# Amplitude copies moved behind their transposes, and the side jobs of a convolution and FFN kernel put in another order

## The chip, the cores and the metric

The kernel runs on one core of a Trainium2 chip. The metric is the device time of one execution in microseconds (us): 1000.81 us before, the median of three runs (998.63 to 1002.74). A core has five engines that run their own instruction streams and wait for one another by semaphores: PE (TensorE, matmuls), DVE (VectorE), ACT (ScalarE, with function tables that must be loaded), POOL (GpSimd) and SP (SyncE, which here issues DMAs).

## What is computed

A block of a sequence model with 2048 rows of 640 columns: a layer norm with a modulation from a condition vector, a convolution with a state-space kernel K (640 channels, 192 modes each), a residual, a second layer norm, and a gated FFN without a nonlinearity (640 to 1536 to 640).

```python
mod = (_silu(c) @ w_mod).reshape(c.shape[0], 6, 1, -1)
sa, ca, ga, sb, cb, gb = (mod[:, i] for i in range(6))
h = _layernorm(x) * (1 + ca) + sa
# _A_ref: dt = exp(log_dt); P = exp(dt * (A_re + 1j*A_im) * l), l = 0..2047
K = jnp.einsum("dn,dnl,dn->dl", Cc, P, dB).real
y = irfft2(rfft2(pad(h)) * rfft2(pad(K)))[:L] + h * Dskip
x = x + ga * y
h = _layernorm(x) * (1 + cb) + sb
x = x + gb * (((h @ w_gate) * (h @ w_up)) @ w_down)
```

## The kernel before

**Generating K.** The 640 channels go in five blocks of 128, db 0 to 4. Each block has two halves, hf 0 to 9, and each half four steps, so that n runs from 0 to 39 (NK = 40). For each n, a value exp(a·l)·sin or cos(b·l) is put together from small tables. `u_seeds(db)` makes the seeds of a block from the inputs A, B and C in steps named by letters: s_d (bit fields of the phase, L689 to L696), s_r (multiples of the decay rate, L702 and L704), s_x, s_e (the exponentials, on ACT), s_f (amplitude `amp` and the input `y` of an arctan, L729 to L734), s_g (transposes of `amp` on PE, then the arctan on ACT), s_h (transposes of the arctan) and s_v (copies of the transposed amplitude into the fourth row of the tile RL, L759, and the phase offset `psi`, L760). The transposes are L639 to L641. The strings SEG0 (block 0) and SEG (the others) group the letters into pieces that are placed one by one.

From the seeds, POOL makes tables: `tab_ph(hf)` the phase table LH (L808 to L814, L789), `tab_eq(hf)` the narrow amplitude table LQ (L823, L824, L789) and, for every n, three outer products on one line, L829: the phases Pha or Phb, EQ (from LQ) and EP (from LP). There are two buffers of each.

**The loop.** `for t in range(3*NK+24)` has three phases per n. ACT takes sines of the phases into the tiles tra and trb (`kg_aq`, `kg_ap`, `kg_b`). DVE multiplies them with EQ and EP to QtA (L884), PtA (L890), PtB (L910) and QtB (L884). PE multiplies these into kg (L925 for the A tiles, L940 for the B tiles), and POOL makes the phases, EQ and EP of n + 1.

**Side jobs.** Everything else is put into this loop as side jobs: seeds of the next block, layer-norm statistics, the modulation, and the convolution itself. Its jobs are `u_pre` (first stage of the input's transform, L986, loads hf), `u_k` (first stage for K, L962), `u_g` and `u_c` (second stages, L1007; `u_c` multiplies the two spectra on DVE, L1048 to L1054, and goes back with L1067) and `u_d` (last stage, L1117 and L1122). Where each piece stands is a number in the table SCHED: 1000 times the half phase of the loop (`due(2t)` stands in front of DVE's multiplies, `due(2t+1)` behind them), plus its place among the jobs there; negative numbers lie in the prologue. The buffers are picked by letters in the table SLOT: `psf` names the PSUM banks a, b and c, `tr` ACT's result tiles, and so on. `mark` and `need` are assertions on the order of the program text; they make no wait. The streams are issued in program order, and semaphores follow from the buffers.

After n = 39 the FFN follows: products of the gate and up weights' halves (L1208) and the down projection (L1624) on PE, with products on DVE and POOL.

Of the kernel before, what the change touches and what calls it, by code (L numbers as in the profile page):

```python
# [14 lines left out]
OP = mybir.AluOpType  # L15
# [17 lines left out]
    ml=(8000, 2001, -93999),  # L33
    mr=(((8004, 13001), (8002, 12000)), ((2002, 8001), (7000, 8003)), ((1, 2000), (-87000, 11004))),
    st=(
        (-96000, -86994),
        (-98000, -86996),
        (2, 12001),
        (2003, 5000),
        (-94999, 4000),  # L40
        (-94000, -86999),
        (14002, 17001),
        (-99999, 0),
        (8005, 8007),
        (-88000, -86995),
        (14003, 18000),
        (8006, 11005),
        (-100000, -86997),
        (-95000, -91000),
        (11000, 11003),  # L50
        (11002, 13002),
    ),
    hm=(
        (29000, 29000),
        (26001, 26001),
        (17000, 17000),
        (32000, 32000),
        (15000, 15000),
        (23000, 23000),
        (22003, 25000),  # L60
        (22001, 27000),
        (35009, 46000),
        (11006, 24002),
        (34000, 36000),
        (32001, 35006),
        (29001, 33000),
        (16001, 20000),
        (43003, 54001),
        (37000, 51002),
    ),  # L70
    rstd=(12002, 18001),
    tab=(52005, 68003),
    fo=(14000, 14001, 14004, 20001),
    e0=(-86998,),
    mc=((11001, 26000, 31002, 34003, 34004), (13000, 35001, 45000, 50000, 51001), (35002, 59000, 63001)),
    q=(
# [4 lines left out]
    ),  # L81
    pre=(
# [8 lines left out]
            (105002, 105004, 108001, 109000),  # L91
            (79000, 81002, 96000, 99000),
            (93001, 93003, 110001, 110002),
            (80001, 82001, 93000, 93002),
        ),
        (
            (139001, 139004, 143000, 144000),
            (132000, 133001, 134010, 139002),
            (119001, 119002, 131000, 132001),
            (111000, 111001, 121000, 123001),  # L100
        ),
        (
            (190003, 192002, 202001, 204000),
            (157000, 157001, 164000, 166002),
            (165000, 167001, 178006, 182004),
            (187003, 187004, 199002, 200000),
        ),
        (
            (207000, 209001, 212001, 215000),
            (220000, 222000, 226000, 229002),  # L110
            (229000, 229001, 232002, 233003),
            (233000, 233004, 236000, 239000),
# [21 lines left out]
        (24001, 26002),  # L134
        (34001, 34002),
        (67001, 69002),
        (51003, 52001),
        (43000, 43004),
        (43002, 46002),
        (52000, 52003),  # L140
        (52002, 52004),
        (66003, 68007),
        (81003, 83000),
        (86002, 92000),
        (108000, 108002),
        (94000, 94001),
        (95000, 95001),
        (105000, 105001),
        (105005, 107000),
        (127000, 127001),  # L150
        (123000, 125006),
        (140000, 144002),
        (134009, 139000),
        (150002, 150004),
        (139003, 140001),
        (150003, 152002),
        (150000, 152001),
        (160001, 162002),
        (166003, 166004),
        (190000, 190002),  # L160
        (192000, 193000),
        (194002, 196000),
        (199001, 199003),
        (196002, 196003),
        (196001, 196004),
# [149 lines left out]
def tile_kernel(ctx: ExitStack, tc: tile.TileContext, I, out):  # L315
# [293 lines left out]
    def u_seeds(db):  # L609
# [22 lines left out]
        T = {}  # L632
# [1158 lines left out]
```

## Time and profile before

| | |
|---|---|
| median of three runs | 1000.81 us (998.63 to 1002.74) |
| the profiled execution | 1001.23 us, of which the span is 999.4 us |
| busy share of the span | PE 90%, DVE 76%, ACT 58%, POOL 58% |
| mean granted TensorE clock | 0.96 of full speed |
| generating K and the convolution | 0 to about 521 us; PE busy 426 us of it |
| FFN | about 521 us to the end; PE busy 468 of 478 us |

Rows of a timeline read: start in us, duration in us (of the whole group, if a count follows as x2), engine, line, operation, the tile written and the tiles read, shapes; in brackets at the end, how long the engine had been idle before it and what ended the idle time. Rows of windows read: start and end, length, then for PE, PEld (weight loads), DVE, ACT and POOL the busy time and the number of instructions, then the granted clock of TensorE, the DMA share and GB/s. A wait's row reads: engine, tile and line that waited, what it waited for, then the total in us, the count and the longest.

### The profile page before, as it was taken

How to read it: one execution, taken by the hardware profiler on the slowest of the kernel's cores; microseconds unless marked ns; L12 is line 12 of the kernel's file. 1: busy time of each engine (PE TensorE's matmuls, PEld its weight loads, DVE VectorE, ACT ScalarE, POOL GpSimd, SP SyncE). 2: the span in 40 equal slices, each digit the busy share in tenths (PEclk: the TensorE clock that was granted, in tenths of full speed). 3: DMA queues.
4: the chain of work that ended last, by engine and by line, in shares of the span. 5: the costliest groups of instructions: out<-in, count | busy, mean ns of one | idle time of the engine just before them, and what ended most of it. 6: DMA issues, size and time to landing. Idle time of an engine off the chain costs nothing.

```text
span 999.4 us, 26670 instructions
## 1 busy us (share of the span) xinstructions
PE 894.6 (90%) x11190; PEld 728.3 (73%) x11190; DVE 760.6 (76%) x1319; ACT 581.7 (58%) x1020; POOL 577.5 (58%) x424
## 2 busy tenths in 40 slices
PE   3966786998798789999878999999999999999998
PEld 2654555775475476677656888889998888889998
DVE  8996678886978977897889877687576877768352
ACT  7789888886978887974564222234463422224331
POOL 5997998799679969970046667650112354442000
PEclk9969999999989979999989999999999999999999
DMA  8756554534365634649741542534645232212341
GB/s 282 280 192 206 167 178 169 159 99 139 108 193 147 178 101 122 183 135 307 223 113 54 192 150 88 185 131 136 224 142 192 101 102 79 80 53 63 95 160 53
DMA packets 141177, 148.96 MB, mean 149 GB/s; under 512 B 8192, under 2 KB 119296, under 8 KB 139648
## 3 DMA queue, kind: packets, MB, share of 16 engines
q1 hardware_dynamic: 139904, 146.32, 46.6%
q8 instruction: 88, 1.44, 0.6%
q10 hardware_dynamic: 1152, 0.92, 0.3%
q14 instruction: 33, 0.27, 0.1%
HBM read 108.36 MB, written 38.86 MB: 147 GB/s over the span
## 4 chain that ended last, share of the span: by engine, by line
PE 64%; ACT 10%; DVE 9%; POOL 7%; issue 5%; DMA 3%; SPq 0%; DVEq 0%; ACTq 0%; POOLq 0%
PE pa L1208 26%; PE pa L1624 16%; PE psfc L1007 2%; PE kg L925 2%; PE kg L940 2%; PE psfa L1007 2%; PE psfb L1007 2%; POOL EQ L829 2%; PE psfa L986 1%; PE psfa L1067 1%; DVE QtA L884 1%; ACT trb L320 1%; ACT tra L320 1%; POOL Phb L829 1%; POOL LH L789 1%
## 5 line engine op out<-in xcount | busy, mean ns | idle before, releaser
L829 POOL TENSOR_TENSOR EQ<-LQ,RH 128x1536 f32<-128x1536 f32 x40 | 124.1, 3102 | 8.5 <-DVE QtB L884 8.3
L320 ACT ACTIVATE z<-pa 128x512 f32<-128x512 f32 x24 | 14.4, 599 | 165.8 <-PE pa L1208 120.1
L1172 DVE TENSOR_TENSOR wsgl<-wga,wsgh 128x640 fp32r<-128x640 f32 x72 | 68.3, 950 | 46.6 <-ACT wsgh L320 46.3
L320 ACT ACTIVATE wsgh<-wga 128x640 fp32r<-128x640 f32 x72 | 52.5, 731 | 72.9 <-PE pa L1624 41.8
L1573 POOL TENSOR_TENSOR z<-z,s 128x512 f32<-128x512 f32 x24 | 33.4, 1391 | 98.8 <-DVE s L1572 98.8
L1624 PE MATMUL pa<-wsgh,sh 128*128 128x384 f32 (+1 forms) x304 | 69.6, 310 | 0.0
L829 POOL TENSOR_TENSOR Pha<-LH,DH 128x1536 int32<-128x1536 int32 x20 | 62.2, 3112 | 12.1 <-ACT tra L320 12.1
L1624 PE MATMUL pa<-wsgl,sh 128*128 128x384 f32 (+1 forms) x304 | 69.2, 309 | 0.0
L1624 PE MATMUL pa<-wsgh,sl 128*128 128x384 f32 (+1 forms) x304 | 69.2, 309 | 0.0
L1184 POOL TENSOR_TENSOR tf<-wur,wgb 128x256 f32<-128x256 f32 x24 | 19.3, 802 | 81.0 <-DVE wtl L1172 54.4
L829 POOL TENSOR_TENSOR EP<-LP,RH 128x768 f32<-128x768 f32 x40 | 66.0, 1649 | 0.0
L829 POOL TENSOR_TENSOR Phb<-LH,DH 128x1536 int32<-128x1536 int32 (+1 forms) x21 | 62.4, 2972 | 3.5 <-ACT trb L320 3.0
L884 DVE TENSOR_TENSOR QtA<-trb,EQ 128x1024 f32<-128x1024 f32 x40 | 47.0, 1215 | 18.9 <-PE kg L925 15.8
L1172 DVE TENSOR_TENSOR wtl<-tf,wth 128x256 fp32r<-128x256 f32 (+1 forms) x72 | 59.9, 859 | 0.0
L884 DVE TENSOR_TENSOR QtA<-tra,EQ 128x1024 f32<-128x1024 f32 x40 | 47.0, 1215 | 13.6 <-ACT tra L320 4.8
L1571 DVE TENSOR_TENSOR s<-pa,s 128x512 f32<-128x512 f32 x24 | 16.6, 691 | 45.1 <-PE pa L1208 40.0
L940 PE MATMUL kg<-QtB,PtB 64*32 64x64 f32 x2560 | 46.5, 224 | 1.4 <-issue 1.0
L1208 PE MATMUL pa<-sl,wth 128*128 128x512 f32 x144 | 45.1, 395 | 2.1 <-DVE sl L1172 2.1
L940 PEld LDWEIGHTS kg<-QtB,PtB 64*32 64x32 f32 x2560 | 39.6, 111 | 9.3 <-issue 6.0
L1624 PEld LDWEIGHTS pa<-wsgh,sh 128*128 128x128 f32 x304 | 46.4, 188 | 0.0
L1624 PEld LDWEIGHTS pa<-wsgh,sl 128*128 128x128 f32 x304 | 46.4, 188 | 0.0
L1624 PEld LDWEIGHTS pa<-wsgl,sh 128*128 128x128 f32 x304 | 46.4, 188 | 0.0
(610 smaller groups left out, 2941.8 us busy)
## 6 DMA issues: line engine op xcount, KB each, us to landing
wga<-wdg SPq DMA_DIRECT2D x24, 640.0 KB, 4.4
wga<-B_w_gate SPq DMA_DIRECT2D x12, 640.0 KB, 5.8
wgb<-B_w_gate SPq DMA_DIRECT2D x24, 320.0 KB, 3.4
wur<-B_w_up SPq DMA_DIRECT2D x24, 320.0 KB, 4.0
xb<-x2d SPq DMA_DIRECT2D x6, 1280.0 KB, 7.2
TVb<-WD SPq DMA_DIRECT2D x20, 256.0 KB, 3.5
t_tw<-w_mod SPq DMA_DIRECT2D x3, 1600.0 KB, 9.2
t_ti<-w_mod SPq DMA_DIRECT2D x3, 1600.0 KB, 8.9
```

Source lines behind the costliest of these rows:

```text
L320: return S.activation(o, i, f, **kw)
L829: G.tensor_tensor(o.rearrange("p x (h l) -> p x h l", l=8), lo.unsqueeze(2).to_broadcast([P, rows, nh, 8]), hi.rearrange("p h x -> p x h") ...
L884: return [lambda h=h: V.tensor_tensor(Qt[:, :, :, 32 * h : 32 * h + 32], tr[:, ::-1] if h else tr[:, :, :, ::-1], e[:, :, 32 * h : 32 * h ...
L925: PE.matmul(kg[j * 32 : j * 32 + 32, dd, :], PtA[:, c, dl * 4 + j, :], QtA[:, c, dl * 4 + j, :], start=dd == 0 and c == 0, stop=False, til ...
L940: PE.matmul(kg[j * 32 : j * 32 + 32, dd, :], PtB[lo : lo + 64, c, r, :], QtB[lo : lo + 64, c, r, :], start=False, stop=dd == 7 and c == 1, ...
L1007: PE.matmul(r[c][par * 64 : par * 64 + 64, i, :], t_tw[:, k0 + k, c, :], src[:, k, :], start=True, stop=True, tile_position=(0, par * 64))
L1172: V.tensor_tensor(lo, v, hi, op=OP.subtract)
L1184: G.tensor_tensor(t[:, 0:2], u[:, 0:2], g[:, 0:2], op=OP.subtract)
L1208: PE.matmul(ps, w[a][:, k], x[b][:, l], start=n == 0 and m == 0, stop=n == 2 and m == len(ks) - 1)
L1571: V.tensor_tensor(S67[i], ps, S6[i], op=OP.add)
L1573: G.tensor_tensor(ZT[i], ZT[i], S67[i], op=OP.add)
L1624: PE.matmul(ACC[tb][t][c], x[:, ts], w[:, cs], start=st, stop=f == NF - 1 and n == 2 and (c == 0 or t % 2 == 1))
```

## The change

Four things change. In `s_f` the amplitude moves from the first to the last place of its six operations. The copies of the transposed amplitude move from `s_v` to `s_g`, directly behind the amplitude's transposes and ahead of the arctan (for block 0 they stood there already, on ACT). `tab_eq` asks for these copies alone (the new mark "amps") and no longer for the whole of the seeds. And nearly all numbers of SCHED and letters of SLOT are others; among them e0, the exponentials of half 1, move from the prologue to the first phase of the loop. Lines from L747 on have a number one higher after the change, so that L884 becomes L885; the five operations behind `amp` become L729 to L733, `amp` L734 and the copies L752.

```diff
-    e0=(-86998,),
+    e0=(2,),
...
-            V.scalar_tensor_tensor(amp, u, dt2[:, db : db + 1], pe[:, 1], op0=OP.mult, op1=OP.mult)
             V.scalar_tensor_tensor(pe[:, 0], pe[:, 0], 1e-37, u, op0=OP.max, op1=OP.add)
             V.reciprocal(pe[:, 0], pe[:, 0])
             V.scalar_tensor_tensor(y, y, 2.0, pe[:, 1], op0=OP.mult, op1=OP.mult)
             V.tensor_tensor(pe[:, 0], y, pe[:, 0], op=OP.mult)
             V.tensor_scalar(y, pe[:, 0], 1.0, -1.0, op0=OP.min, op1=OP.max)
+            V.scalar_tensor_tensor(amp, u, dt2[:, db : db + 1], pe[:, 1], op0=OP.mult, op1=OP.mult)
...
                 for h in range(2):
                     act(g4(Rl[h])[:, 3], T["ps2"][:, 0, hs[h]])
+                mark("amps", db)
...
             if db:
                 s_G()
+                for h in range(2):
+                    V.tensor_copy(g4(Rl[h])[:, 3], T["ps2"][:, 0, hs[h]])
+                mark("amps", db)
             act(y, y, AF.Arctan)
...
             ps = T["ps2"]
-            if db:
-                for h in range(2):
-                    V.tensor_copy(g4(Rl[h])[:, 3], ps[:, 0, hs[h]])
             V.tensor_scalar(psi, ps[:, 1], 4294967296.0 / math.pi, 536870912.0, op0=OP.mult, op1=OP.add)
...
-        need(1, "seeds", hf // 2)
+        need(1, "amps", hf // 2)
```

What the new numbers do is shown at three places.

The first is ACT at n = 13, where the seeds of block 2 are made. `ab`, `tra` and `trb` are the sines' tiles, `ptb` and `psfa` the square root and absolute value of the seeds, LP, RH and RL the exponentials. Before:

```order
L320 ACTIVATE gha<-psfb 128x512
L320 ACT_TABLE_LOAD
L320 ACTIVATE ptb<-ptb 128x192
L320 ACTIVATE psfa<-ptb 128x192
L320 ACT_TABLE_LOAD
L320 ACTIVATE LP<-RL 128x192 x7
L320 ACTIVATE RH<-RH 128x2112
L320 ACTIVATE RL<-RL 128x2x288
L320 ACTIVATE ab<-Pha 128x512
L320 ACT_TABLE_LOAD
L320 ACTIVATE tra<-Pha 128x512
L320 ACTIVATE tra<-ab,halfpi 128x512
```

And now:

```order
L320 ACTIVATE ab<-Phb 128x512
L320 ACTIVATE trb<-Phb 128x512
L320 ACTIVATE trb<-ab,halfpi 128x512
L320 ACT_TABLE_LOAD
L320 ACTIVATE ptb<-ptb 128x192
L320 ACTIVATE psfc<-ptb 128x192
L320 ACT_TABLE_LOAD
L320 ACTIVATE LP<-RL 128x192 x7
L320 ACTIVATE RH<-RH 128x2112
L320 ACTIVATE RL<-RL 128x2x288
```

The third set of sines of n = 13 has moved from behind the exponentials to a place ahead of them and of the square root. On DVE, at the same n, the first of the two product groups (six operations each) has moved ahead of L714, and `amp` stands last of its group; both product groups still stand ahead of PtB and QtB.

The second place is DVE at n = 22, where the seeds of block 3 are finished (`psfa` and `psfc` are PSUM banks, `prm` holds `amp`, `pta` the arctan's input and TVb the spectra's product). Before, from L714 to the copies:

```order
L714 TENSOR_SCALAR psfa<-ptb 128x192
L884 TENSOR_TENSOR QtA<-trb,EQ_144 128x32x32 x2
L1048 TENSOR_TENSOR TVb<-psfb,gha 128x512
...
L1054 TENSOR_TENSOR TVb<-TVb,psfc 128x512
L729 SCALAR_TENSOR_TENSOR prm<-ptb,dt_100,psfa 128x192
L730 SCALAR_TENSOR_TENSOR psfa<-psfa,ptb 128x192
L731 RECIPROCAL psfa<-psfa 128x192
L732 SCALAR_TENSOR_TENSOR pta<-pta,psfa 128x192
L733 TENSOR_TENSOR psfa<-pta,psfa 128x192
L734 TENSOR_SCALAR pta<-psfa 128x192
L759 COPY RL<-psfa 128x96 x2
L760 TENSOR_SCALAR ptb<-psfa 128x192
```

And now, from QtA on:

```order
L885 TENSOR_TENSOR QtA<-tra,EQ_144 128x32x32 x2
L1049 TENSOR_TENSOR TVb<-psfb,ghc 128x512
...
L1055 TENSOR_TENSOR TVb<-TVb,psfa 128x512
L714 TENSOR_SCALAR psfc<-ptb 128x192
L729 SCALAR_TENSOR_TENSOR psfc<-psfc,ptb 128x192
L730 RECIPROCAL psfc<-psfc 128x192
...
L733 TENSOR_SCALAR pta<-psfc 128x192
L734 SCALAR_TENSOR_TENSOR prm<-ptb,dt_100,psfc 128x192
L752 COPY RL<-psfc 128x96 x2
L891 TENSOR_TENSOR PtAb<-trb,EP_146 128x1024
L761 TENSOR_SCALAR ptb<-psfc 128x192
```

L714 has moved behind QtA and the product group, `amp` to the end of its group, and PtA stands between the copies and psi.

The third place is n = 29, where the seeds of block 4 are finished, on DVE and on PE. On DVE, before:

```order
L890 TENSOR_TENSOR PtAa<-trb,EP_147 128x1024
L714 TENSOR_SCALAR psfa<-ptb 128x192
L729 SCALAR_TENSOR_TENSOR prm<-ptb,dt_100,psfa 128x192
...
L734 TENSOR_SCALAR pta<-psfa 128x192
L910 TENSOR_TENSOR PtB<-tra,EP_147 128x512
L884 TENSOR_TENSOR QtB<-tra,EQ_145 128x16x32 x2
L884 TENSOR_TENSOR QtA<-trb,EQ_144 128x32x32 x2
L759 COPY RL<-psfa 128x96 x2
```

And now:

```order
L891 TENSOR_TENSOR PtAa<-tra,EP_147 128x1024
L911 TENSOR_TENSOR PtB<-trb,EP_147 128x512
L885 TENSOR_TENSOR QtB<-trb,EQ_145 128x16x32 x2
L714 TENSOR_SCALAR psfc<-ptb 128x192
L1123 TENSOR_TENSOR xsa<-psfa,xsa 128x512
...
L734 SCALAR_TENSOR_TENSOR prm<-ptb,dt_100,psfc 128x192
L885 TENSOR_TENSOR QtA<-tra,EQ_144 128x32x32 x2
L752 COPY RL<-psfa 128x96 x2
```

PtB and QtB of n = 29 have moved ahead of L714 and the six operations. On PE, behind the L1117 group of n = 28, before:

```order
L940 MATMUL kg<-QtB,PtB 32x64 x32
L1117 MATMUL psfa<-TVb,ct 32x512 x4
L1007 MATMUL psfc<-ghc,t_tw 64x128 x2
...
L1067 MATMUL psfb<-TVa,t_ti 128x128
L925 MATMUL kg<-QtA,PtAa 32x64 x32
L929 MATMUL kg<-dsel,jsel 128x8
```

And now:

```order
L1118 MATMUL psfa<-TVb,ct 32x512 x4
L926 MATMUL kg<-QtA,PtAa 32x64 x32
L930 MATMUL kg<-dsel,jsel 128x8
L1008 MATMUL psfb<-ghb,t_tw 64x128 x2
...
L941 MATMUL kg<-QtB,PtB 32x64 x32
L1068 MATMUL psfc<-TVa,t_ti 128x128
```

The L925 block of n = 29 has moved ahead of the L1007 block, and the L1067 block to a place behind L940; the amplitude's transposes (L639) come behind these as before.

More of the change, by code (lines that the diff above doesn't have):

```diff
@@ L133 @@
     k=(
[L134 to L146, printed above, removed]
-        (95000, 95001),
[L148 to L165, printed above, removed]
-        (208001, 211001),
-        (233001, 237000),
-        (220001, 224005),
-        (229003, 229004),
+        (20000, 25000),
+        (35010, 36002),
+        (67008, 68000),
+        (53000, 57000),
+        (40001, 42002),
+        (40000, 43001),
+        (56001, 59000),
+        (52000, 53001),
+        (67004, 67005),
+        (82002, 82003),
+        (90001, 93000),
+        (104000, 107000),
+        (95000, 95001),
+        (96000, 96001),
+        (103003, 105000),
+        (103006, 106000),
+        (128002, 128003),
+        (128000, 128001),
+        (143000, 143001),
+        (136000, 140000),
+        (156000, 156002),
+        (140002, 140004),
+        (148000, 150000),
+        (159000, 159003),
+        (160000, 162002),
+        (169000, 169001),
+        (187004, 190000),
+        (189001, 193000),
+        (203000, 203001),
+        (200000, 200001),
+        (198000, 198001),
+        (196000, 197000),
+        (210002, 210004),
+        (233004, 233005),
+        (220000, 224000),
+        (231000, 231001),
         (287007, 287017),
@@ L175 @@
     low=(
-        (15001, 43005, 64000, 90003, 110000, 139005, 160000, 187005, 211002),
-        (16000, 43001, 68000, 90005, 116000, 136000, 162000, 187002, 211000),
+        (14000, 43000, 66000, 88005, 115001, 136003, 162001, 187005, 206000),
+        (16000, 42000, 67007, 88003, 112000, 136001, 164001, 187003, 209001),
     ),
```

130 lines of the change are left out of this document (65 added, 65 removed), and 34 rows, old and new, of tables (d, g, pre, q).

## The prediction

> **What bounds the kernel now.** I read the chain of waits first, then the windows, then the list of POOL's waits, then the timeline at the five places where seeds are made. The chain ends on PE:
>
> ```profile
> PE 64%; ACT 10%; DVE 9%; POOL 7%; issue 5%; DMA 3%; SPq 0%; DVEq 0%; ACTq 0%; POOLq 0%
> ```
>
> The windows (start, length, then busy time and count of PE, PEld, DVE, ACT, POOL) show where that holds:
>
> ```profile
> 25.00:75.00 50.00, 39.88 (x641) 30.91 (x640) 46.58 (x108) 42.10 (x70) 49.13 (x28) 0.80 0.69 236
> 75.00:120.00 45.00, 31.32 (x618) 21.87 (x620) 27.84 (x43) 42.14 (x67) 38.87 (x26) 0.93 0.56 181
> 375.00:521.00 146.00, 131.02 (x2620) 99.26 (x2620) 117.72 (x229) 97.84 (x166) 77.24 (x48) 0.96 0.59 177
> 521.00:999.00 478.00, 468.35 (x2464) 411.92 (x2462) 338.29 (x532) 170.81 (x330) 179.95 (x162) 0.99 0.38 122
> ```
>
> From 521 us on PE is busy 468.35 of 478, and the diff leaves that part's order alone: it can only move as a block. Before it, POOL (49.13 of 50) and then ACT (42.14 of 45) are fuller than PE, and each n must pass POOL's EQ and EP. So what the change is worth is the sum of POOL's waits that go or come before its last EP, unless PE cannot follow. POOL's largest waits in the table stage are (total, times, longest):
>
> ```profile
> POOL LQ L823 <- DVE RL L759: 14.2, 3, 9.6
> POOL Pha L829 <- ACT tra L320: 12.1, 4, 7.6
> POOL EQ L829 <- DVE QtB L884: 8.3, 4, 4.5
> ```
>
> The narrow table LQ waits for the amplitude copies three times; that is the wait the change aims at. All work stays the same but one ACT_TABLE_LOAD more; the rest is order.
>
> **Start, db 0.** The edit puts amp last in the group of six:
>
> ```profile
> 13.96 0.41 DVE L729 SCALAR_TENSOR_TENSOR prm<-ptb,dt,psfa 128x192 f32<-128x192 f32 x1
> 17.00 0.36 DVE L734 TENSOR_SCALAR pta<-psfa 128x192 f32<-128x192 f32 x1
> 19.95 0.35 DVE L760 TENSOR_SCALAR ptb<-tra 128x192 int32<-128x192 f32 x1
> ```
>
> Amp was ready at 13.96 + 0.41 = 14.37 and will be at 17.36, 3.0 us later; the arctan's input comes 0.4 us sooner, which helps nobody, because ACT has amp's copies and a table load in front of the arctan. So the arctan and its transposes come about 3.0 us later.
>
> ```profile
> 17.39 0.36 ACT L320 ACTIVATE pta<-pta 128x192 f32<-128x192 f32 x1
> 17.77 1.28 ACT L320 ACT_TABLE_LOAD   x1
> 20.70 1.43 ACT L320 ACTIVATE LP<-RL 128x96 f32<-128x96 f32 x7 [1.64 <-DVE RL L702]
> 21.92 1.08 ACT L320 ACTIVATE RH<-RH 128x1056 f32<-128x1056 f32 x1
> 22.90 0.42 ACT L320 ACTIVATE RL<-RL 128x288 f32<-128x288 f32 x1
> 18.70 0.32 PE L641 MATMUL tra<-ct,pta 128*64 128x64 f32 x1
> 20.57 0.39 POOL L765 TENSOR_TENSOR DL<-ptb 128x96 int32<-128x96 int32 x1
> ```
>
> The arctan's transposes end at 19.02; 3.0 later is 22.0, so psi (19.95 before) slips 2.05, and it had 0.27 to spare before POOL's L765 at 20.57: POOL starts its phases **1.8 us later**. Half 1's exponentials (1.43 + 1.08 + 0.42 = 2.93) go behind the first sines, which costs the added table load, 1.28. POOL is full from 25 to 75, so it carries the 1.8 along. Its first waits for ACT, near 75, could swallow it, but ACT itself is the longer by 1.28. I take +1.8; the ends are 0 (swallowed) and 1.8 + 1.28 = +3.1.
>
> The Trainium skill ("ScalarE: Activation LUTs", What ACT_TABLE_LOAD costs) puts a switch of tables at 1283 ns for the load and about 1380 ns for a drain, 2.66 us together. The trace disagrees on the second part: the load issued at 170.71, shown under db 2, takes 1.28 and the exponentials begin at 172.01, 1.30 after it. By the page the sum would be 1.4 us worse.
>
> **db 1.** One row decides:
>
> ```profile
> 97.30 0.36 POOL L823 COPY LQ<-RL 128x96 f32<-128x96 f32 x1 [1.91 <-DVE RL L759]
> ```
>
> The copies now follow amp's transposes and no longer stand behind the arctan, its transposes and psi's place on DVE. One table load (1.28), one arctan (0.36) and a set of transposes no longer precede them. In db 0 the transposes take from the arctan's end, 17.75, to 19.02, 1.3 us. Together 2.9 us, more than 1.91. I take **-1.9**, between that and 0.
>
> **db 2, n = 13.** ACT's exponentials held back the trig that frees the phase buffer:
>
> ```profile
> 170.71 1.28 ACT L320 ACT_TABLE_LOAD   x1
> 172.01 2.63 ACT L320 ACTIVATE LP<-RL 128x192 f32<-128x192 f32 x7
> 178.79 0.60 ACT L320 ACTIVATE tra<-Pha 128x512 f32<-128x512 int32 x1
> 182.46 1.28 DVE L884 TENSOR_TENSOR QtB<-tra,EQ 128x512 f32<-128x512 f32 x2
> 179.54 3.11 POOL L829 TENSOR_TENSOR Pha<-LH,DH 128x1536 int32<-128x1536 int32 x1 [7.61 <-ACT tra L320]
> 183.88 3.11 POOL L829 TENSOR_TENSOR EQ<-LQ,RH 128x1536 f32<-128x1536 f32 x1 [1.22 <-DVE QtB L884]
> ```
>
> The trig now comes first, so the 7.61 goes. But the next EQ needs its buffer back from QtB, which ended at 183.74, and on DVE both product groups (L1048 to L1054) and the six amplitude operations still stand ahead of it. So EQ waits to about the same moment: 7.61 + 1.22 becomes one wait of about 8.8 one row later. I take **0**, between -7.6 (QtB comes early too) and +1.4 (what QtB loses if the second product group waits for its shared bank; the nearest row is that EQ wait of 1.22).
>
> **db 3, n = 22.**
>
> ```profile
> 268.50 0.36 DVE L714 TENSOR_SCALAR psfa<-ptb 128x192 f32<-128x192 f32 x1 [1.90 <-ACT psfa L320]
> 268.78 2.34 DVE L884 TENSOR_TENSOR QtA<-trb,EQ 128x1024 f32<-128x1024 f32 x2
> 280.65 0.42 DVE L759 COPY RL<-psfa 128x96 f32<-128x96 f32 x2 [2.45 <-PE psfa L641]
> 281.04 0.36 POOL L823 COPY LQ<-RL 128x96 f32<-128x96 f32 x1 [9.58 <-DVE RL L759]
> ```
>
> L714 goes behind QtA and the product group, so DVE need not sit 1.90 us for ACT: QtA and the products start about 1.9 earlier. L714 then adds 0.36 in front of the reciprocal. The copies' own wait of 2.45 was for the arctan's transposes. They now need amp's alone; but amp itself is ready only where the arctan's input was, at the end of its group, so no more than the second set of transposes, 1.3, is left to gain. Together 1.9 - 0.36 + 1.3 = **2.8 us** of the 9.58, since POOL has nothing else to wait for. The ends are 0 and -9.6.
>
> **db 4, n = 29.**
>
> ```profile
> 351.24 1.21 DVE L890 TENSOR_TENSOR PtAa<-trb,EP 128x1024 f32<-128x1024 f32 x1
> 356.06 0.68 DVE L910 TENSOR_TENSOR PtB<-tra,EP 128x512 f32<-128x512 f32 x1
> 356.65 1.28 DVE L884 TENSOR_TENSOR QtB<-tra,EQ 128x512 f32<-128x512 f32 x2
> 365.10 0.42 DVE L759 COPY RL<-psfa 128x96 f32<-128x96 f32 x2 [0.37 <-PE psfa L641]
> 358.08 3.10 POOL L829 TENSOR_TENSOR EQ<-LQ,RH 128x1536 f32<-128x1536 f32 x1 [4.55 <-DVE QtB L884]
> 365.49 0.36 POOL L823 COPY LQ<-RL 128x96 f32<-128x96 f32 x1 [2.71 <-DVE RL L759]
> 360.27 1.93 PE L925 MATMUL kg<-QtA,PtAa 128*32 128x64 f32 x64
> 363.61 0.49 PE L639 MATMUL psfa<-ct,prm 128*128 128x128 f32 x2
> 350.00:356.00 6.00, 3.26 (x28) 2.88 (x28) 5.79 (x10) 5.99 (x12) 3.53 (x2) 0.50 0.17 67
> ```
>
> PtB and QtB move ahead of L714 and the six (3.4 us from 13.96 to 17.36; 3.7 with L714): EQ starts 3.7 of its 4.55 sooner. On PE the block L925 of n = 29 passes the L1007 and L1067 blocks, so PE idles until PtA is ready (351.24 + 1.21 = 352.45) and L925 starts there, not at 360.27. From L925 to amp's transposes it is 3.34 us (360.27 to 363.61); now the two passed blocks lie between. The L1007 block is most of the 3.26 busy in the window row, at a granted clock of 0.50; L1067 is about as long, an estimate from its like number of matmuls. So amp's transposes start at 352.45 + 3.34 + 6.5 = 362.3 if the clock stays at 0.50 and at 359.1 if it is full, 1.3 to 4.5 us sooner. I take 2.0, near the cold end, because the idle stretch ahead of L925 grows. The copies need only the first set of transposes, worth 0.6 more. So LQ starts **2.6 us** earlier and that is the stage's gain: 3.7 appears at EQ, and 1.1 of it returns as a longer wait at LQ. The ends are 0 and 4.55 + 2.71 = -7.3.
>
> **The rest.** Other jobs change places with their neighbours, and all ring letters change; per n the sum of each engine's work shifts by a few us and is level again at n = 39. On SP the loads of hf, gh and TV go with their jobs; DMA is 3% of the chain, and no wait on a DMA stands among the three above. A ring letter can add a wait where none is shown: in 375 to 521 PE has 146 - 131.02 = 15 us of gaps that could grow or shrink. I take 0 for all of it; the ends are +-4.5, the longest single wait of EQ on QtB, as one more such wait or one less.
>
> **Sum.** 1.8 - 1.9 + 0 - 2.8 - 2.6 = -5.5. The profiled execution took 1001.23 us (999.4 of span and 1.8 around it), 0.4 above the median of 1000.81. 1001.2 - 5.5 = **995.7**, and the three runs before lie 4 us apart (998.63 to 1002.74), which hides the 0.4. That is 0.5% below the median, about what a measurement of this kernel can tell from no change: 5 us either way counts as the same.
>
> **Rivals.**
> - *The wait of 7.61 is not replaced.* If QtB of n = 13 comes early, since DVE loses its 1.90-like pauses there too, db 2 gives -7.6 on top: 988. For it: POOL had nothing else to wait for. Against: DVE is packed from 171 to 184 with the same operations.
> - *The change does not reach the end.* LQ is bound to the copies alone, but the copies still follow the six operations, and amp is last of them. If POOL's EQ waits take over each time, or PE's blocks fill up from 375 on (131.02 of 146) before POOL's lead arrives, the time stays within 999 to 1003, say 1001. For it: db 2, where exactly this exchange happens.
> - *ACT becomes the bound from the start.* Place: 25 to 120 us. Moved into ACT's loop are 2.93 of exponentials and 1.28 of table load, with seeds 2.05 late: 6.3 us. ACT has 50 - 42.10 = 7.9 idle in the first window, but much of that is waiting for DVE, and only 45 - 42.14 = 2.9 in the next. From the point where less than 6.3 of those 7.9 can be filled the remainder stays for good, db 1's LQ finds ACT late and gains nothing, and POOL is late everywhere. Price: +6.3 instead of +1.8, 0 instead of -1.9, and the later gains shrunk to the 1.3 of the transposes in db 3: +5.0, so 1006. Against: the sines of n = 0, which free the first multiplies, go ahead by as much as the exponentials go back.
>
> **How the numbers follow.** My forecast (993 to 998.7) has 0.43, split about evenly by the 995.8 that lies 0.5% below the median; the first rival (986 to 993) 0.20; the second (998.7 to 1003) 0.21; the third 0.16, nearly all of it beyond +0.5%. So faster by over 0.5% is 0.22 + 0.20 = 0.42; within 0.5% is 0.21 + 0.21 + 0.01 = 0.43; slower 0.15. The range 988 to 1005 leaves out about half of each outer rival, and holds the ends of the unknown terms taken one at a time.
>
> **What would show it.** db 0: POOL's L765 near 22.4. db 1: POOL's LQ without a wait, before 97. db 2: no wait of Pha, and a wait of some 8 us at EQ for QtB in its place. db 3: L714 behind the products, LQ's wait near 7. db 4: EQ's wait under 1 and LQ's near 4, one PE gap of over 8 us ahead of L925. The last EP about 5 us earlier and the last 478 us unchanged. It is wrong if POOL's waits go and the FFN does not begin earlier, or if ACT shows no idle time before 120 us.

## The result, and the profile after

The changed kernel took 988.31 us (median of six runs, 985.82 to 992.44), against 1001.44 us (998.38 to 1007.43, six runs) for the kernel before: a ratio of 0.987, with a 95% interval of 0.983 to 0.991. It is 13 us faster, where 5.5 were forecast; the time lies in the range of 988 to 1005, 0.3 us above its low end, which is also the first rival's time. The profiled execution is one of the longer ones, 992.28 us with a span of 990.5, 8.95 below the one before. The stages below are read from these two.

The chain of the changed kernel still ends on PE. POOL's share fell from 7% to 4%, those of DVE and ACT rose:

```profile
PE 63%; DVE 12%; ACT 12%; issue 5%; POOL 4%; DMA 2%; SPq 1%; DVEq 0%; ACTq 0%; POOLq 0%
```

Its windows at the places shown before (the end moved up by 10 us):

```profile
25.00:75.00 50.00, 42.12 (x653) 30.98 (x653) 45.68 (x101) 46.57 (x80) 49.45 (x29) 0.90 0.65 208
75.00:120.00 45.00, 36.44 (x758) 26.02 (x756) 33.59 (x58) 43.48 (x71) 43.03 (x29) 0.89 0.64 209
375.00:521.00 146.00, 130.22 (x2466) 99.04 (x2463) 116.40 (x223) 98.76 (x168) 71.59 (x48) 0.98 0.60 181
521.00:989.00 468.00, 459.70 (x2426) 404.95 (x2424) 330.50 (x524) 164.77 (x320) 173.88 (x159) 1.00 0.37 121
```

ACT's busy time (the fourth) rose from 42.10 to 46.57 in the first window, and POOL's (the fifth) from 38.87 to 43.03 in the second. Most of ACT's rise is half 1's exponentials, which ran ahead of 25 us before and now run from 24.96 to 27.60, and the added table load (1.28). Counted from 0 to 75 us ACT's busy time rose by 3.3, from 59.71 to 63.01, and 2.0 of that is not the table load: ACT's work was moved forward, and POOL waits less behind it. POOL's waits up to 443 us (total, times, longest) in the changed kernel:

```profile
POOL EQ L830 <- DVE QtB L885: 13.2, 3, 10.2
POOL LQ L824 <- DVE RL L752: 8.9, 3, 5.8
...
POOL Phb L830 <- ACT trb L320: 2.2, 3, 0.9
POOL Pha L830 <- ACT tra L320: 1.5, 2, 0.8
```

LQ's waits fell from 14.2 to 8.9 and Pha's from 12.1 to 1.5, but EQ's wait for QtB rose from 8.3 to 13.2. The timeline of POOL in the changed kernel shows where, at its L766 in db 0 and then at EQ and LQ of the other blocks:

```profile
22.38 0.39 POOL L766 TENSOR_TENSOR DL<-ptb 128x96 int32<-128x96 int32 x1 [0.94 <-POOL ptb L765]
...
93.72 0.36 POOL L824 COPY LQ<-RL 128x96 f32<-128x96 f32 x1 [0.66 <-DVE RL L752]
...
170.02 3.11 POOL L830 TENSOR_TENSOR Phb<-LH,DH 128x1536 int32<-128x1536 int32 x1 [0.60 <-ACT trb L320]
183.30 3.10 POOL L830 TENSOR_TENSOR EQ<-LQ,RH 128x1536 f32<-128x1536 f32 x1 [10.18 <-DVE QtB L885]
...
274.43 0.36 POOL L824 COPY LQ<-RL 128x96 f32<-128x96 f32 x1 [5.77 <-DVE RL L752]
...
347.01 3.12 POOL L830 TENSOR_TENSOR EQ<-LQ,RH 128x1536 f32<-128x1536 f32 x1
...
354.17 0.35 POOL L824 COPY LQ<-RL 128x96 f32<-128x96 f32 x1 [2.43 <-DVE RL L752]
```

The start of EQ for each n is a good clock for the whole stage. It gives the lead of the changed kernel over the one before (start after minus start before, us; negative is earlier):

| up to EQ of | before | after | lead | this stage |
|---|---|---|---|---|
| n = 0 | 25.42 | 27.21 | +1.8 | +1.8 (start) |
| n = 5 | 69.89 | 71.66 | +1.8 | 0 |
| n = 8 | 108.80 | 107.11 | -1.7 | -3.5 (db 1) |
| n = 12 | 151.75 | 147.12 | -4.6 | -2.9 (behind db 1) |
| n = 15 | 183.88 | 183.30 | -0.6 | +4.1 (db 2) |
| n = 20 | 237.68 | 237.20 | -0.5 | +0.1 |
| n = 24 | 292.67 | 285.93 | -6.7 | -6.3 (db 3) |
| n = 30 | 345.78 | 339.30 | -6.5 | +0.3 |
| n = 32 | 377.00 | 365.65 | -11.4 | -4.9 (db 4) |
| n = 39 | 438.01 | 426.53 | -11.5 | -0.1 |

Nearly all of the gain is waits that went: between EQ of n = 0 and of n = 39 POOL waited 38.7 us before and 25.8 after. From EQ of n = 5 to EQ of n = 12 POOL waited 7.25 us before and 1.42 after, and from n = 20 to n = 24 it was 15.32 and 9.23. Before, these rows stood there beside LQ's waits:

```profile
75.71 3.11 POOL L829 TENSOR_TENSOR Phb<-LH,DH 128x1536 int32<-128x1536 int32 x1 [1.11 <-ACT trb L320]
84.64 3.10 POOL L829 TENSOR_TENSOR Pha<-LH,DH 128x1536 int32<-128x1536 int32 x1 [1.16 <-ACT tra L320]
89.47 3.09 POOL L829 TENSOR_TENSOR EQ<-LQ,RH 128x1536 f32<-128x1536 f32 x1 [1.72 <-DVE QtB L884]
...
251.96 3.11 POOL L829 TENSOR_TENSOR Phb<-LH,DH 128x1536 int32<-128x1536 int32 x1 [1.85 <-ACT trb L320]
262.80 3.11 POOL L829 TENSOR_TENSOR Pha<-LH,DH 128x1536 int32<-128x1536 int32 x1 [3.06 <-ACT tra L320]
266.75 3.10 POOL L829 TENSOR_TENSOR EQ<-LQ,RH 128x1536 f32<-128x1536 f32 x1 [0.83 <-DVE QtB L884]
```

And now, in the same two stages:

```profile
102.81 3.11 POOL L830 TENSOR_TENSOR Pha<-LH,DH 128x1536 int32<-128x1536 int32 x1 [0.76 <-ACT tra L320]
...
258.30 3.11 POOL L830 TENSOR_TENSOR Phb<-LH,DH 128x1536 int32<-128x1536 int32 x1 [0.93 <-ACT trb L320]
263.94 3.12 POOL L830 TENSOR_TENSOR EQ<-LQ,RH 128x1536 f32<-128x1536 f32 x1 [2.53 <-DVE QtB L885]
```

At n = 29 PE stands still until PtA is ready:

```profile
343.18 1.93 PE L926 MATMUL kg<-QtA,PtAa 128*32 128x64 f32 x64 [8.32 <-DVE PtAa L891]
```

Of the 11.5 us, 8.9 reach the end of the span. The stretch from EQ of n = 39 to the end, whose order is the same in all kernels but for a few rows at its start, took 561.4 us before and 564.0 after, and between 561.3 and 565.7 in the twelve profiles of the experiments below. So what it gave back is no more than what it varies by.

### The profile page after: what moved, and what is told of

Same layout as the page of the kernel before. It is cut to its first block, busy times and chain, and to the rows that moved or that the text cites. A ratio compares the mean times of both kernels' runs of the same rounds, so it can differ in the third digit from the quotient of the medians.

```text
span 990.5 us, 26674 instructions
## 1 busy us (share of the span) xinstructions
PE 888.0 (90%) x11190; PEld 722.2 (73%) x11190; DVE 761.5 (77%) x1319; ACT 582.1 (59%) x1021; POOL 576.8 (58%) x424
## 4 chain that ended last, share of the span: by engine, by line
PE 63%; DVE 12%; ACT 12%; issue 5%; POOL 4%; DMA 2%; SPq 1%; DVEq 0%; ACTq 0%; POOLq 0%
PE pa L1209 26%; PE pa L1625 16%; PE psfc L1008 2%; PE kg L941 2%; PE psfb L1008 2%; PE kg L926 2%; PE psfb L963 2%; DVE QtA L885 1%; PE psfb L1068 1%; ACT trb L320 1%; PE psfa L1008 1%; DMA t_tw<-w_mod 1%; PE psfa L987 1%; ACT tra L320 1%; DVE QtB L885 1%
## 5 line engine op out<-in xcount | busy, mean ns | idle before, releaser
L830 POOL TENSOR_TENSOR EQ<-LQ,RH 128x1536 f32<-128x1536 f32 x40 | 124.3, 3108 | 13.3 <-DVE QtB L885 13.2
L830 POOL TENSOR_TENSOR Phb<-LH,DH 128x1536 int32<-128x1536 int32 x20 | 62.4, 3118 | 2.2 <-ACT trb L320 2.2
L830 POOL TENSOR_TENSOR Pha<-LH,DH 128x1536 int32<-128x1536 int32 (+1 forms) x21 | 62.5, 2975 | 2.0 <-ACT tra L320 1.5
L885 DVE TENSOR_TENSOR QtA<-tra,EQ 128x1024 f32<-128x1024 f32 x40 | 47.0, 1216 | 13.0 <-ACT tra L320 6.6
L885 DVE TENSOR_TENSOR QtA<-trb,EQ 128x1024 f32<-128x1024 f32 x40 | 47.0, 1215 | 10.7 <-ACT trb L320 4.7
```

The costliest lines, as they stand in the source:

```text
L830: G.tensor_tensor(o.rearrange("p x (h l) -> p x h l", l=8), lo.unsqueeze(2).to_broadcast([P, rows, nh, 8]), hi.rearrange("p h x -> p x h") ...
L885: return [lambda h=h: V.tensor_tensor(Qt[:, :, :, 32 * h : 32 * h + 32], tr[:, ::-1] if h else tr[:, :, :, ::-1], e[:, :, 32 * h : 32 * h ...
```

## The experiments

Eleven variants ran, and the changed kernel once more, each beside the kernel before on the same chip. Ratios are to that kernel, with the 95% interval. The numbers edited are those of SCHED; where several were edited, the diff shows them in one line, with "..." for numbers left as they were. "EQ 15" stands for the start of EQ for n = 15.

**The edits of the code alone.** The changed code with the tables SCHED and SLOT of before.

> The edits of the code alone (amp last, copies directly behind amp's transposes) with the numbers and ring letters of before. Theory A, the gain is one of order: the edits give little by themselves. The start loses 1.8 us at POOL; the copies need only amp's transposes, which takes at most 1.3 us off LQ's wait at each of db 1, 3 and 4; sum between -2 and +2, so 999 to 1003 us, and POOL's last EQ within 2 us of 438.0. Theory B, the gain comes from the copies' new place: POOL's last EQ 6 us or more earlier, 995 us or less.

Measured: 1004.74 us, ratio 1.006 (1.002 to 1.009): slower, if by little. Stage by stage the profile shows what the copies' new place is worth: EQ 5 to EQ 8 takes 36.37 us instead of 38.91 (part of it the late start, which is absorbed there), EQ 22 to EQ 24 36.41 instead of 37.63, EQ 30 to EQ 32 29.41 instead of 31.22. That is about the 1.3 per block that was expected. But EQ 20 to EQ 22 took 21.54 instead of 17.36. No instruction stands in another order there: on all five engines the rows of this kernel are those of before, but for amp's place (the copies keep their row on DVE too; what falls away is their wait for the arctan's transposes). POOL waits there for ACT, 6.03 us at the phases in front of EQ 22 instead of 1.85. What differs ahead of it is the clock granted to a PE that is busy 55 to 56 of 60 us. The same window of the kernel before, and of the code alone:

```profile
180.00:240.00 60.00, 56.36 (x1267) 41.63 (x1255) 48.85 (x68) 49.10 (x85) 57.76 (x39) 0.97 0.43 126
```

```profile
180.00:240.00 60.00, 55.23 (x1150) 40.33 (x1140) 46.08 (x64) 44.47 (x76) 56.55 (x39) 0.89 0.42 124
```

0.97 became 0.89 (the third figure from the end). That ACT and POOL lost their time to this clock is likely, but not shown, and whether the edits cause the lower clock, one profile doesn't tell; that the edits alone don't carry the gain is shown. Theory B falls. Theory A has the direction, but its bounds were missed: 1004.74 us against 999 to 1003, and a last EQ at 441.06, 3.1 behind 438.0.

**The copies back behind the arctan.**

```diff
             if db:
                 s_G()
-                for h in range(2):
-                    V.tensor_copy(g4(Rl[h])[:, 3], T["ps2"][:, 0, hs[h]])
-                mark("amps", db)
             act(y, y, AF.Arctan)
...
             ps = T["ps2"]
+            if db:
+                for h in range(2):
+                    V.tensor_copy(g4(Rl[h])[:, 3], ps[:, 0, hs[h]])
+                mark("amps", db)
```

At db 2 and db 3 the numbers of s_v and LQ were moved by one or two places within their phase, so that LQ stands behind the copies.

> The changed kernel with the copies back behind the arctan's transposes, in front of psi, and LQ right behind them. Theory A (order): the copies move to psi's place, 1.5 us later at db 3 (274.04 to 275.5), 1.3 at db 4 (353.78 to 355.1) and about 2 at db 1; the last EQ comes 3 to 5 us later than 426.5 and stays 6 us or more ahead of 438.0. Theory B (copies): the gain at db 1, 3 and 4 falls away, and the last EQ is within 3 us of 438.

Measured: 990.39 us, ratio 0.992 (0.990 to 0.995). The last EQ came at 426.06, as early as in the changed kernel, where 3 to 5 us later were expected, though the copies cost nearly what they should: 1.3 us at EQ 8 (108.43 against 107.11), LQ's wait at db 3 7.05 instead of 5.77, at db 4 3.14 instead of 2.43. It was ahead elsewhere, at EQ 15 (181.06 against 183.30); a section below says why. With the copies in their old place the order still gives most of the gain. Amp stands last in this run; the next one puts it first. No run has the new order with both edits undone.

**Amp first again.**

```diff
+            V.scalar_tensor_tensor(amp, u, dt2[:, db : db + 1], pe[:, 1], op0=OP.mult, op1=OP.mult)
             V.scalar_tensor_tensor(pe[:, 0], pe[:, 0], 1e-37, u, op0=OP.max, op1=OP.add)
...
             V.tensor_scalar(y, pe[:, 0], 1.0, -1.0, op0=OP.min, op1=OP.max)
-            V.scalar_tensor_tensor(amp, u, dt2[:, db : db + 1], pe[:, 1], op0=OP.mult, op1=OP.mult)
```

> The changed kernel with amp first of its six operations again. Theory A1, amp's last place costs: amp is ready 3.0 us sooner, its transposes lie beside the reciprocal, the start wins back 1.8 us at POOL's L766, and the copies at db 3 and db 4 lose their waits of 0.86 and 0.90 us for PE; the last EQ comes 2 to 4 us before 426.5 and the time falls by as much. Theory A2, amp's last place is what makes the arctan come early: putting it first delays the arctan's input by 0.4 us at each block and wins nothing; last EQ at 426.5 within 1 us.

Measured: 987.44 us, ratio 0.990 (0.986 to 0.993), not to be told from the changed kernel. The start did not move: EQ 0 at 27.24. The timelines of ACT, DVE and POOL in this kernel show why:

```profile
17.23 0.36 ACT L320 ACTIVATE pta<-pta 128x192 f32<-128x192 f32 x1
...
20.68 0.35 DVE L696 TENSOR_TENSOR ptb<-psfa,shl 128x192 int32<-128x192 int32 x1
20.95 0.87 DVE L580 BATCH_NORM_STATS2 st<-f16a 128x6 f32<-128x320 f32 x2
21.85 0.21 DVE L581 BATCH_NORM_AGGREGATE mv<-st 128x2 f32<-128x12 f32 x1
21.98 0.31 DVE L761 TENSOR_SCALAR ptb<-trb 128x192 int32<-128x192 f32 x1
...
22.43 0.38 POOL L766 TENSOR_TENSOR DL<-ptb 128x96 int32<-128x96 int32 x1 [0.93 <-POOL ptb L765]
...
178.13 3.11 POOL L830 TENSOR_TENSOR EQ<-LQ,RH 128x1536 f32<-128x1536 f32 x1 [7.92 <-DVE QtB L885]
```

The arctan comes at 17.23, as early as in the kernel before, and psi (L761) still at 21.98: three batch-norm statistics, which stand ahead of psi on DVE with the new numbers (one did before), fill the time. The copies at db 3 and db 4 still wait 0.86 and 0.90 us for PE, so the gains that theory A1 counted on did not come. The last EQ was at 422.99, 3.5 earlier, but this lead arose between EQ 12 (146.94 against 147.12) and EQ 15 (178.13 against 183.30), before amp of block 2 is needed by LQ.

**Amp first, and the statistics behind psi.**

```diff
-    (-93000, -92999), (-91000, -90999), (-90998, -89000)
+    (-93000, -87993), (-91000, -87992), (-90998, -87991)
```

> The changed kernel with amp first and three batch-norm statistics moved behind psi on DVE. Psi then stands directly behind its bit fields: POOL's L766 comes near 19.9 instead of 22.4 and EQ of n = 0 near 25 instead of 27.2. Theory K, ACT sets the pace up to db 1: POOL's lead of 2 us is gone by EQ of n = 8, which stays within 0.5 of 106.9, and the time does not move; then the prediction's term for the start belongs in the sum with 0. Theory L, the lead is carried: EQ of n = 8 near 104.7 and 2 us less at the end.

Measured: 989.80 us, ratio 0.990 (0.987 to 0.993). POOL's rows:

```profile
20.08 0.39 POOL L766 TENSOR_TENSOR DL<-ptb 128x96 int32<-128x96 int32 x1
...
24.90 3.10 POOL L830 TENSOR_TENSOR EQ<-LQ,RH 128x1536 f32<-128x1536 f32 x1
...
94.81 0.36 POOL L824 COPY LQ<-RL 128x96 f32<-128x96 f32 x1 [3.46 <-DVE RL L752]
...
107.50 3.10 POOL L830 TENSOR_TENSOR EQ<-LQ,RH 128x1536 f32<-128x1536 f32 x1
```

POOL started 2.3 us earlier, waited 3.46 at LQ of db 1, and had nothing left at EQ 8 (107.50, 0.6 from 106.9 where theory K allowed 0.5). Theory K holds: what the start wins or loses is gone by db 1. The last EQ came at 428.26, about 2 us later than in the changed kernel: db 4 (EQ 30 to EQ 32) took 29.35 us instead of 26.35, which was not followed up.

**Half 1's exponentials back in the prologue.**

```diff
-    e0=(2,),
+    e0=(-86998,),
```

> The changed kernel with half 1's exponentials back in the prologue, ahead of the first sines, and one table load less. Theory G, psi alone sets POOL's start: its L766 stays at 22.4 and its EQ of n = 0 at 27.2, and the last EQ and the time stay within 1 us. Theory H, the sines of n = 0 have to stand first: they come 2.9 us later, POOL's phases of n = 2 or 3 wait for them, and the last EQ comes 1 to 3 us later.

Measured: 985.03 us, ratio 0.987 (0.981 to 0.993); the changed kernel itself, run again beside it, 988.18 and 0.988 (0.982 to 0.995). EQ 0 at 27.15, EQ 8 at 107.62, the last EQ at 424.89. POOL's start stayed, as theory G has it; the last EQ and the median came 1.3 and about 3 us earlier than in the changed kernel beside it, more than the 1 us that theory G allowed, but the intervals overlap almost wholly. No effect that can be measured, for or against, and nothing of theory H. The table load added at the start costs nothing that shows.

**Four normalizations back behind n = 2.**

```diff
-        (15000, 15000), (15003, 15003), (16004, 16004), (15001, 15001),
+        (24002, 24002), (25002, 25002), (27002, 27002), (28002, 28002),
```

> The changed kernel with four of the normalizations on ACT (0.8 us each) moved from n = 2 back to n = 4, near the place where the kernel before had them. Theory M, the gain at db 1 is ACT work moved ahead into idle time: ACT comes to db 1 about 3 us later, EQ of n = 7 or LQ of db 1 waits again, and EQ of n = 8 comes 2 to 4 us later than 106.9. Theory N, db 1 gains from the copies' place and the order of the seeds there: EQ of n = 8 within 0.7 of 106.9.

Measured: 991.82 us, ratio 0.990 (0.986 to 0.994). ACT's busy time between 25 and 75 us fell from 46.57 to 43.93. POOL:

```profile
95.73 0.36 POOL L824 COPY LQ<-RL 128x96 f32<-128x96 f32 x1 [2.22 <-DVE RL L752]
...
109.52 3.10 POOL L830 TENSOR_TENSOR EQ<-LQ,RH 128x1536 f32<-128x1536 f32 x1
```

EQ 8 came at 109.52, against 106.83 in the changed kernel's second profile (106.83 to 107.62 in all others with the new order and the copies in their new place). Of those 2.7 us, 2.5 were still there at EQ 24 (287.35 against 284.85). Theory M holds: ACT's work, moved ahead into time when it had been idle, is what db 1 gains from, for these 2.7 us. The copies' place, which theory N names, is worth another 1.3 there by the run with the copies back.

**The order at db 2.** Two edits: the second product group and the six operations of s_f behind PtB and QtB of n = 13 (db2_late), and the product group alone (db2_c2).

```diff
-            (79002, 82007, 92000, 93003),
+            (79002, 83001, 92000, 93003),
...
-        (..., 82000, 82001, 82006, 87000, 88002, 88004),
+        (..., 82000, 82001, 83000, 87000, 88002, 88004),
```

> The changed kernel with the six amplitude operations and the second product group of n = 13 put behind PtB and QtB. Theory C, db 2 is bound by the seeds' chain and not by QtB: EQ's wait of 10.18 us shrinks to about 3, but a wait of 6 us or more appears at LQ, since the copies end near 187 as before, and the last EQ moves by less than 1.5 us. Theory D, QtB alone is what POOL waits for at db 2: the lead of 4.6 us that POOL had ahead of db 2 is kept and grows, and the last EQ comes 5 us or more before 426.5.

> The changed kernel with the second product group of n = 13 alone put behind PtB and QtB; the six operations stay ahead. Theory C, the seeds' chain binds db 2: EQ's wait falls by 4 us, from 10 to 6, a wait of 2 to 3 us appears at LQ, and EQ of n = 16 moves by 1 us at most. Theory D, QtB alone binds: EQ of n = 16 comes 4 us earlier than in a run at the same granted clock.

Measured: 995.86 us, ratio 0.997 (0.994 to 1.001), with both, and 995.06 us, 0.996 (0.994 to 0.999), with the first line alone. POOL with the product group alone behind:

```profile
176.14 3.09 POOL L830 TENSOR_TENSOR EQ<-LQ,RH 128x1536 f32<-128x1536 f32 x1 [5.88 <-DVE QtB L885]
...
186.23 0.36 POOL L824 COPY LQ<-RL 128x96 f32<-128x96 f32 x1 [5.39 <-DVE RL L752]
...
198.18 3.11 POOL L830 TENSOR_TENSOR EQ<-LQ,RH 128x1536 f32<-128x1536 f32 x1
```

And with both:

```profile
176.28 3.08 POOL L830 TENSOR_TENSOR EQ<-LQ,RH 128x1536 f32<-128x1536 f32 x1 [5.63 <-DVE QtB L885]
...
189.74 0.36 POOL L824 COPY LQ<-RL 128x96 f32<-128x96 f32 x1 [8.78 <-DVE RL L752]
...
201.26 3.11 POOL L830 TENSOR_TENSOR EQ<-LQ,RH 128x1536 f32<-128x1536 f32 x1
```

EQ's wait fell from 10.18 to under 6, and a wait as long came up at LQ, which waits for the copies. What that did to EQ 16 has to be read against a run with the same clock: these two had 0.66 between 140 and 150 us, the two profiles of the changed kernel 0.50. The kernel with db 4's order undone, described below, has the changed kernel's order up to here, and 0.66 too:

```profile
179.82 3.10 POOL L830 TENSOR_TENSOR EQ<-LQ,RH 128x1536 f32<-128x1536 f32 x1 [9.54 <-DVE QtB L885]
...
195.94 3.10 POOL L830 TENSOR_TENSOR EQ<-LQ,RH 128x1536 f32<-128x1536 f32 x1
```

Against it EQ 15 comes 3.7 and 3.5 us earlier, and EQ 16 (198.18 and 201.26) 2.2 and 5.3 later. Theory D falls. Theory C has the mechanism, that what QtB gives is lost at the copies, but not the sizes: LQ waits 5.39 where 2 to 3 were expected, and EQ 16 moves by more than 1. Both kernels lost more behind db 2 (last EQ at 429.1 and 429.4), which was not followed up.

**The seeds of block 2 one phase earlier.** If the seeds' chain binds db 2, moving it ahead should help.

```diff
-        (..., 82000, 82001, 82006, 87000, 88002, 88004),
+        (..., 81000, 82001, 82002, 84000, 85000, 85003),
...
-            (79002, 82007, 92000, 93003),
+            (79002, 83001, 92000, 93003),
```

> The changed kernel with the later seeds of block 2 moved ahead by one phase each and the second product group of n = 13 put behind PtB and QtB. Theory C, the seeds' chain binds db 2: the wait of EQ of n = 15 falls by about 4 us and no wait of the same size comes at LQ, because the copies and psi come earlier too; the last EQ comes 3 to 5 us earlier than that of the changed kernel in the same call and the time falls by as much. Theory D, QtB alone binds: putting the six operations behind PtB and QtB already gave all that is to be had, EQ of n = 16 is not before 198.

Measured: 1001.54 us, ratio 1.001 (0.998 to 1.004): the whole gain was lost. EQ 15 came at 177.16, as expected, with a wait of 1.17, and none came at LQ; but the phases in front of EQ 15 and EQ 16 waited 4.96 and 2.17 us for ACT's sines, and EQ 16 came at 197.65, 1.7 later than in the kernel with db 4's order undone, at nearly the same clock (0.65 and 0.66). POOL then waited 2.7 us at EQ 17 and 2.0 at EQ 19, and EQ 20 was at 242.48 instead of 237.20. So the expectation failed at db 2 too. ACT loads a table 27 times in this kernel instead of 26, since the seeds' operations are now split by a set of sines; how much that accounts for isn't settled. That the seeds' chain alone binds db 2 is not shown: QtB, the copies and ACT's sines lie close behind one another there.

**DVE's order at db 4 undone.**

```diff
-        (..., 179001, 179002, 179004, 182001, ...),
+        (..., 178000, 178001, 178002, 182001, ...),
```

> The changed kernel with the six amplitude operations at n = 29 ahead of PtB and QtB on DVE again. The prediction's step: EQ of n = 31 waits 3.5 to 4.5 us for QtB again; LQ's wait shrinks by 1 to 2, and the last EQ comes 2 to 3 us later. The rival: the copies' chain sets db 4, EQ's wait moves but EQ of n = 32 stays within 0.5 us.

Measured: 992.69 us, ratio 0.993 (0.990 to 0.996). POOL, and the copies on DVE:

```profile
345.14 3.09 POOL L830 TENSOR_TENSOR EQ<-LQ,RH 128x1536 f32<-128x1536 f32 x1 [1.61 <-DVE QtB L885]
...
353.84 0.36 POOL L824 COPY LQ<-RL 128x96 f32<-128x96 f32 x1 [4.00 <-DVE RL L752]
...
353.44 0.42 DVE L752 COPY RL<-psfa 128x96 f32<-128x96 f32 x2 [4.09 <-PE psfa L641]
```

EQ 30 to EQ 32 took 29.56 us instead of 26.35: the order is worth 3.2 of the stage's 4.9. The loss stands elsewhere than was expected: 1.61 at EQ, and LQ's wait grew from 2.43 to 4.00 instead of shrinking. The copies waited 4.09 for amp's transposes. On PE these come behind the L1008 block of n = 29, and that block stood 2.87 us for a result of DVE, L1123, which the six operations hold back as they hold back QtB:

```profile
344.91 0.68 DVE L1123 TENSOR_TENSOR xsa<-psfa,xsa 128x512 f32<-128x512 f32 x1
345.65 0.69 PE L1008 MATMUL psfa<-ghb,t_tw 128*64 128x128 f32 x4 [2.87 <-DVE xsa L1123]
```

So the place of the six operations sets both of POOL's waits, one through QtB and the other through L1123 and PE. The rival, by which EQ 32 would not move, falls. The last EQ came at 426.19, no later than in the changed kernel, since this run was 2.4 to 3.5 us ahead of it at EQ 30 (335.76) for the reason given in the last section.

**The changed kernel again, and two parts undone together.**

> The changed kernel once more, beside the three below on one chip. Its profile at db 2 was taken at a granted clock of 0.83 from 120 to 180 us; the two runs of it with the code's edits undone reached EQ of n = 15 at 178 and 181 us instead of 183. Theory E, a low clock of TensorE in that stretch cost the profiled run some 3 us: this profile shows EQ of n = 15 before 181 and a last EQ before 424. Theory F, the edits set it: EQ of n = 15 at 183 again and the last EQ at 426.5 within 1.

Measured: 988.18 us, ratio 0.988 (0.982 to 0.995). The second profile got the same low clock, 0.83 between 120 and 180 us, and EQ 15 at 181.96, the last EQ at 426.18. So this run alone doesn't decide between E and F; the other kernels do, below.

> The changed kernel with amp first and half 1's exponentials back in the prologue, the two undone parts that did not make it slower. Theory I, neither part carries a gain: the time is that of the changed kernel, 0.985 to 0.990 of the kernel before, and no version so far beats it. Theory J, each part wins its 1 to 3 us: 0.983 or less.

Measured: 992.22 us, ratio 0.992 (0.989 to 0.995). Theory J falls. The ratio lies even a little above the 0.985 to 0.990 of theory I; db 4 took 29.28 us here, as in the run with the early start. No version beats the changed kernel by more than the runs vary.

## Why the prediction was right, point by point

- **The way was right**: faster, through POOL's waits ahead of its last EQ, and the FFN moved as a block. Its sum of -5.5 stands against -11.5 at the last EQ, -8.95 in the profiled execution and -13 in the medians. That the time still fell into the range is luck: three stages gave 10.3 us more than was forecast, db 2 took 4.1 back, and the low end of 988 came from a rival whose mechanism did not occur.
- **Start, +1.8.** L766 was to come near 22.4 and came at 22.38. The figure was right and its cause only half: the arctan did slip by 2.8, but the statistics hold psi back to the same moment without it (the run with amp first). And the term belonged in the sum with 0: db 1 absorbs it, as the run with the early start showed with the other sign. This was the low end that the prediction named and did not take.
- **db 1, -1.9.** The step that was most mis-sized. From EQ 5 to EQ 12 the lead changed by 6.4 us. The prediction said that one row decides, LQ's wait, and that row gave only 1.25 (1.91 fell to 0.66). It left out the small waits around it, for ACT, QtB and a load (5.34 before, 0.76 after), because it put the other jobs that "change places with their neighbours" at 0. They did not only change places: ACT did 2.0 us more work before 75 us, table load aside, and four of the moved operations alone account for 2.7.
- **db 2, 0.** The mechanism was right: Pha's 7.61 went and a wait at EQ took its place. In the profiled execution its size was not: 10.18 where 8.8 was forecast, with EQ 15 only 0.6 ahead after a lead of 4.6 at n = 12, a loss of 4.1 beyond the end of +1.4. The end came from a wait on a shared bank and left out that PE's own pace in between could change. With amp first, at a clock of 1.00 from 140 to 150 us, the wait was 7.92 and the stage gave 0.9 (31.19 us from EQ 12 to EQ 15, 32.13 before), near the forecast; the 5 us between the two profiles are the clock and the pause of the last section.
- **db 3, -2.8.** LQ's wait fell by 3.8 (9.58 to 5.77) and the stage by 6.3. L714, the reciprocal and the copies went as worked out, and the copies' place gave the 1.3 that was counted for it (LQ's wait 7.05 with the copies back): from QtB to the copies it took 10.5 us instead of 14.1. What was missed lies ahead: the waits of the phases in front of EQ 22 and EQ 23, 1.85 and 3.06, fell to 0 and 0.93, while EQ 23's own rose from 0.83 to 2.53. No experiment took this part of db 3 apart, so which of the moves brought it stays open.
- **db 4, -2.6.** The stage gave 4.9, and DVE's order alone 3.2. EQ's wait of 4.55 went altogether. PE stood still for 8.3 us ahead of L926, as forecast, and ran on at a granted clock of 0.56 from 342 to 348. LQ's wait was 2.43 and not near 4: counted from EQ 30, amp's transposes came 4.2 us sooner, where the sum took 2.0 "near the cold end" of 1.3 to 4.5; the clock was 0.50 from 340 to 347 us and 1.00 from 348 to 354, where most of the L1068 block lies.
- **The rivals.** The first had the time, though not the way: db 2 did not give 7.6. The second, that waits change places, is true of db 2 alone. The third, ACT as the bound from the start, did not come: here the late start did not add up, it was absorbed by db 1.

## What to carry to other kernels

Follow one engine's start times through both traces, step by step: the table of leads located within a stage what the sum of waits hid, and showed which leads are lost again. A wait that is removed is worth only what the next wait behind it leaves; at db 2 three kernels took some 4 us or more off EQ and lost them at LQ, at the phases or later. Before an edit is credited with a lead, compare the granted clock and the pauses of both profiles in the stage where the lead arises. Where a change reorders small jobs of an engine that is full in one stage and idle in the stage ahead, work out what was moved between these two, however alike the rows look.

## What the hardware showed unasked

Executions with the same order of work reached EQ 15 at different times, by the clock that was granted to PE and by a pause of PE. Up to that point the rows of the changed kernel, of amp first and of the undone db 4 are alike, but for amp's place, and EQ 12 comes within 0.2 us in all three (147.12, 146.94, 147.04). In the changed kernel the window from 140 to 150 us:

```profile
140.00:150.00 10.00, 8.60 (x56) 4.57 (x50) 5.86 (x15) 3.34 (x7) 9.76 (x8) 0.50 0.66 189
```

And with amp first:

```profile
140.00:150.00 10.00, 7.81 (x210) 6.54 (x206) 9.54 (x21) 7.32 (x15) 9.77 (x8) 1.00 0.75 211
```

At a clock of 0.50 PE fell behind (the 16 matmuls of the first L963 block took 1.92 us instead of 1.04), its L1008 block at n = 13 began at 163.26 instead of 159.21, and EQ 15 came at 183.30 instead of 178.13; the undone db 4, with 0.66 there, lies between at 179.82. Not all of this is the clock. Just before, PE stood still in the changed kernel in the middle of a block, for nothing that the profile shows:

```profile
138.94 0.61 PE L926 MATMUL kg<-QtA,PtAb 128*32 128x64 f32 x11 [2.21 <-issue]
```

With amp first it did not. The two can be told apart by the run with the early start, the changed kernel's second profile and its first: all had 0.50 between 140 and 150 us, and pauses there of 0.35, 1.05 and 2.21. From EQ 12 to EQ 15 they took 34.42, 35.08 and 36.18 us, so the pause goes in nearly one for one; amp first, at 1.00 and without a pause, took 31.19. That leaves about 3 of the 5 us for the clock and 2 for the pause, an estimate from these four profiles. Whether the pause brings on the low clock they don't show; the run with 0.35 got it too.

The lead of amp first at the last EQ (3.5 us) is this and not the edit: the early start, which has amp first too, reached EQ 15 at 181.97, as late as the changed kernel's second profile (181.96). It may account for part of the 6.6 us by which the six runs of one kernel differ. The Trainium skill ("TensorE: Matmul & The Clock Gate", What's actually happening) says that the gate's activity window runs freely, so that the same kernel meets it differently from run to run, and puts the penalty of the ramp at under 1% of a typical kernel's span. The traces agree in size, about 3 us in 990 by the estimate above, though here it arises in the middle of the span.
